# Linear attention and a snake MLP on one core: reading q of the first chunk in 2-KB rows

## The chip, the core and the metric

The kernel runs on one core of a Trainium2 chip. The core has a matrix engine (TensorE, "PE" in the profile; "PEld" is its loading of weights), a vector engine (VectorE, DVE), a scalar engine (ScalarE, ACT), GpSimd (POOL) and SyncE (SP). Each of them works through its own queue of instructions in order. Transfers between the chip's memory and the core's SBUF are issued by SP, ACT or POOL and carried out by 16 DMA engines that all of them share. TensorE writes its results to PSUM, eight banks of 512 fp32 columns in 128 partitions.

The metric is the device time of one execution in microseconds (us), the median of several runs.

## What is computed

Two stages follow one another. The first is a linear attention with decay, over 4 batches, 8 heads, 768 tokens and 64 features to a head, written for blocks of 64 tokens:

```python
for b in range(nb):
    intra = np.einsum('bhic,bhjc->bhij', qb, kb) * Dmask[None]
    intra = np.einsum('bhij,bhjd->bhid', intra, vb)
    inter = np.einsum('bhid,bhde->bhie', qb * lam_pow[None], kv_state)
    out[:, :, sl] = intra + inter
    kv_state = lam_block * kv_state + np.einsum('bhsd,bhse->bhde', kb * rev_pow, vb)
```

`Dmask`, `lam_pow` and `rev_pow` are powers of a decay `lam` that each head has for itself. The second is an MLP on the 3072 x 512 result (heads side by side), with 2048 hidden features:

```python
h = x @ w_in
s = np.sin(alpha * h)
g = h + s * s / (alpha + 1e-09)
return g @ w_out
```

All inputs and the output are fp32; the kernel works in bf16 with fp32 sums.

## The kernel before

The sequence is cut into six chunks of 128 tokens. For each chunk t the kernel makes `xt[t]`, the attention's output for the 4 x 128 tokens of all batches, with features in partitions; then the MLP's first half (`hidden`, 16 steps of four products of 512 columns, line 468), the snake (line 471 on ScalarE, line 485 on VectorE), and the second half (`project`, line 496), whose units are woven into the `hidden` steps of the next chunk. There is no scheduler: the order in the code is the order in each engine's queue.

Loads of q, k, v and the weights are issued by GpSimd, because they turn fp32 into bf16 on the way (`load`, lines 95 to 104; `load_w_in`, line 89; `load_w_out`, line 92). A load of one batch of q, k or v for one chunk puts tokens in partitions: partition p gets token p of eight heads, 64 features each, so it is 1024 pieces of 64 elements, 256 bytes read and 128 written. Batch 0's k and q come as fp32 through SP (line 81) and are cast on ScalarE and VectorE. Lines 112 to 120 issue, in this order: k and q of batches 1, 2 and 3, v of batches 0 to 3, `w_in` in two halves of its first quarter and then its three other quarters. `w_out`'s first quarter is issued in line 585, and the rest between the loads of the next chunk (lines 591, 629 and 630).

The first chunk has a code of its own (lines 544 to 582), with one mask over 128 tokens and no state yet. For each batch:

- `turn` (line 284) turns k and q with four transposes on TensorE (line 288) into one PSUM bank, of which they use half as bf16; ScalarE copies it to `QKT` (line 290). `turn_in_two` (line 277) does it for q of batch 0 with two copies. The layout wanted is features in partitions (two heads of 64 one above the other), four pairs of heads, 128 tokens in order.
- `scores1` (line 309) multiplies k and q of each head (line 313), and VectorE multiplies the sums with the decay mask `C0` into `STm` (line 317).
- `outs` multiplies with v (line 324), and ScalarE (batch 0, line 329) or VectorE (batches 1 to 3, with the decay `Etab`, line 331) writes `xt[0]`.

`spin` (line 127) issues products on a constant tile whose results nobody reads. Between these steps ScalarE works out small tables of powers of the decay: `decay_64` (`NE64` and `R64`, line 170), `decay_of_pair` (`L64`, line 195), `decay_128`, and `etab` (line 200). `mask_table` and `decay_k` on GpSimd, and the states of later chunks, use them.

At the end, `store` (line 500) copies a finished 128 x 512 tile out of PSUM and issues it on SP (`put_held`, line 514), in one transfer, or in two of 256 columns for the last chunk. The very last tile goes through `project_last` (line 516): 384 columns, a copy, two stores of 256 and 128 columns; then 128 columns, a copy, a store.

Of the kernel before, what the change touches and what calls it, by code (L numbers as in the profile page):

```python
# [15 lines left out]
def kernel(  # L16
# [11 lines left out]
    nc = tc.nc  # L28
    P = nc.NUM_PARTITIONS

    B, H, S, D = q.shape
    T = 128
    NT = S // T
    HP = H // 2
# [23 lines left out]
    def bank(nm, n, dtype=FP32):  # L58
        return psum.tile([P, 512 if dtype is FP32 else 1024], dtype, name=nm, tag=f"b{n}")
# [11 lines left out]
    qn, kn, vn = {}, {}, {}  # L71
    NAT = {"k": (kn, k), "q": (qn, q), "v": (vn, v)}

    def new_chunk(t):
        for d, nm, p in ((qn, "qn", qkp), (kn, "kn", qkp), (vn, "vn", vp)):
            d[t] = p.tile([P, B, H, D], BF16, name=nm)
# [18 lines left out]
    def load(t, nm, b0, b1):  # L95
        dst, src = NAT[nm]
        to = dst[t][:, b0:b1, :, :].rearrange("p b h e -> p (b h) e")
        by_head = src[b0:b1, :, t * T:(t + 1) * T, :].rearrange("b h p e -> p (b h) e")
        n = H * (b1 - b0)
        if t and nm != "v" and b0 == 2:  # L100
            nc.gpsimd.dma_start(out=to[:, 0:n - 1, :], in_=by_head[:, 1:n, :])  # L101
            nc.gpsimd.dma_start(out=to[:, n - 1:n, :], in_=by_head[:, 0:1, :])
        else:
            nc.gpsimd.dma_start(out=to, in_=by_head)  # L104

    new_chunk(0)
    new_chunk(1)

    dist = consts.tile([P, T], FP32, name="dist")
    nc.gpsimd.iota(out=dist[:], pattern=[[1, T]], base=0, channel_multiplier=-1,  # L110
                   allow_small_or_imprecise_dtypes=True)
    for nm, b0, b1 in (("k", 1, 2), ("q", 1, 2), ("k", 2, 3), ("q", 2, 3), ("k", 3, 4), ("q", 3, 4),
                       ("v", 0, 1), ("v", 1, 2), ("v", 2, 3)):
        load(0, nm, b0, b1)
    for hs in (slice(0, HP), slice(HP, H)):
        nc.gpsimd.dma_start(out=vn[0][:, 3, hs, :], in_=v[3, hs, 0:T, :].rearrange("h p e -> p h e"))  # L116
    load_w_in(0, 0, 2 * P)
# [9 lines left out]
    def spin(n, bk, cols=256):  # L127
        ps = bank("hps", bk)
        for _ in range(n):
            nc.tensor.matmul(out=ps[:, 0:cols], lhsT=fill[:, 0:P], rhs=fill[:, 0:cols], start=True, stop=True)  # L130

    iden = consts.tile([P, P], BF16, name="iden")
# [35 lines left out]
    def powers(nm, n, src, shape):  # L168
        t = consts.tile(shape, FP32, name=nm)
        nc.scalar.activation(out=t[:], in_=src, func=ACTF.Exp, scale=pcol[:, n:n + 1])  # L170
        return t
# [17 lines left out]
    def decay_64():  # L189
        later["NE64"] = powers("NE64", 3, lnlam[:].rearrange("p (hp hd) -> p hd hp", hd=2), [P, 2, HE])  # L190
        later["R64"] = powers("R64", 4, lnlam[:], [P, H + 2])

    def decay_of_pair(pr):
        for hd, half in enumerate(HALF):
            nc.scalar.activation(out=L64[half, pr, :], in_=lnlam[half, pr + hd:pr + hd + H - 1:2],
                                 func=ACTF.Exp, scale=float(D))
# [13 lines left out]
    V, G, A = nc.vector, nc.gpsimd, nc.scalar  # L210
    xt = {}
    kdec = {}
    KT, QT, both = {}, {}, {}
# [63 lines left out]
    def turn_in_two(t, b, n):  # L277
        ps = bank("T_ps", n, BF16)[:].rearrange("p (n c i) -> p n c i", n=2, c=HP)[:, 1]
        for hp in range(HP):
            nc.tensor.transpose(out=ps[:, hp, :], in_=qn[t][:, b, 2 * hp:2 * hp + 2, :], identity=iden[:])  # L280
        nc.scalar.copy(out=both[t][:, 1, b, 0:2, :], in_=ps[:, 0:2])
        nc.vector.tensor_copy(out=both[t][:, 1, b, 2:4, :], in_=ps[:, 2:4])

    def turn(t, nm, b, n, eng):
        src, u = (kn, 0) if nm == "k" else (qn, 1)
        ps = bank("T_ps", n, BF16)[:].rearrange("p (n c i) -> p n c i", n=2, c=HP)[:, u]
        for hp in range(HP):
            nc.tensor.transpose(out=ps[:, hp, :], in_=src[t][:, b, 2 * hp:2 * hp + 2, :], identity=iden[:])  # L288
        if eng is nc.scalar:
            eng.copy(out=both[t][:, u, b, :, :], in_=ps)  # L290
        else:
            eng.tensor_copy(out=both[t][:, u, b, :, :], in_=ps)
# [16 lines left out]
    def scores1(t, b, ns):  # L309
        Fb = [bank("F0_ps", n)[:].rearrange("p (c i) -> p c i", c=HP) for n in ns]  # L310
        for hp in range(HP):
            for hd in range(2):
                nc.tensor.matmul(out=Fb[hd][:, hp, :], lhsT=KT[t][halves(hd), b, hp, :],
                                 rhs=QT[t][halves(hd), b, hp, :], start=True, stop=True)
        st = work.tile([P, 2, HP, T], BF16, name="STm")
        for hd in range(2):
            nc.vector.tensor_tensor(out=st[:, hd], in0=Fb[hd], in1=C0[:, hd], op=ALU.mult)
        STm[t, b] = st
# [170 lines left out]
    held = []  # L489
# [10 lines left out]
    def store(g, m):  # L500
        o_sb = outp.tile([P, DM], FP32, name="o_sb")
        if g < NT - 2 and (g or m < 3):
            nc.vector.tensor_copy(out=o_sb[:], in_=ops_of.pop((g, m))[:])  # L503
        else:
            nc.scalar.copy(out=o_sb[:], in_=ops_of.pop((g, m))[:])  # L505
        held.append((m * S + g * T, o_sb, 2 if g == NT - 1 else 1))
        if g:
            put_held()

    def put_held():  # L510
        while held:
            row, o_sb, n = held.pop(0)
            for c in range(0, DM, DM // n):
                nc.sync.dma_start(out=out[row:row + T, c:c + DM // n], in_=o_sb[:, c:c + DM // n])

    def project_last(g, m):
        for n, (c, c1) in enumerate(((0, 3 * P), (3 * P, DM))):
            cols = slice(c, c1)
            ps = bank("hps", HB[n])
            for f in range(NFC):  # L520
                nc.tensor.matmul(out=ps[:, 0:c1 - c], lhsT=gall[g][:, f, m * P:(m + 1) * P],  # L521
                                 rhs=w_out_sb[f // 4][:, f % 4, cols],
                                 start=(f == 0), stop=(f == NFC - 1))
            o_sb = outp.tile([P, DM], FP32, name="o_sb")
            nc.scalar.copy(out=o_sb[:, 0:c1 - c], in_=ps[:, 0:c1 - c])
            row = m * S + g * T
            for c0 in range(c, c1, 2 * P):
                e = min(c0 + 2 * P, c1)
                nc.sync.dma_start(out=out[row:row + T, c0:e], in_=o_sb[:, c0 - c:e - c])

    new_xt(0)
    new_turned(0)
# [3 lines left out]
    def mask_128(hd):  # L536
        nc.vector.tensor_tensor(out=C0[:, hd], in0=tri[:].unsqueeze(1).broadcast_to([P, HP, T]),
                                in1=NE[:, hd].unsqueeze(2).broadcast_to([P, HP, T]), op=ALU.mult)
# [2 lines left out]
    nc.vector.tensor_tensor(out=qn[0][:, 0, :, :], in0=raw["q0"][:], op=ALU.mult,  # L541
                            in1=Rq[:].unsqueeze(2).broadcast_to([P, H, D]))
    mask_128(1)
    turn(0, "k", 0, 4, A)
    spin(2, 3)
    turn_in_two(0, 0, 5)
    spin(2, 3)
    turn(0, "k", 1, 1, A)
    scores1(0, 0, (6, 7))
    turn(0, "q", 1, 2, A)  # L550
    nc.sync.dma_start(out=alpha_fp[:], in_=moe_alpha.rearrange("(f p) -> f p", p=P))
    turn(0, "k", 2, 0, A)
    decay_64()
    spin(1, 3)
    scores1(0, 1, (4, 5))
    turn(0, "q", 2, 1, A)
    decay_of_pair(0)
    spin(1, 3)
    turn(0, "k", 3, 2, A)
    spin(1, 3)  # L560
    scores1(0, 2, (6, 7))
    turn(0, "q", 3, 0, A)
    a_ps = bank("a_ps", OB)
    nc.tensor.transpose(out=a_ps[:, 0:NFC], in_=alpha_fp[:], identity=idf[:])
    alpha_sb = consts.tile([P, NFC], FP32, name="alpha_sb")
# [40 lines left out]
    def queue_units(g, order):  # L606
        for m, part in order:
            def unit(g=g, m=m, part=part):
                project(g, m, part)
                if part == 3:  # L610
                    store(g, m)
            behind.append(unit)
# [69 lines left out]
    def slots(g):  # L682
        t = g + 1
        d = {i: [] for i in range(NFC)}
        if g == 1:
            at = dict(KV=5, F=9, O=12)
        else:
            at = dict(KV=4, F=8, O=12)
        d[at["KV"]] += [(states, t)]
        for n in range(4):  # L690
            d[at["KV"] + ((0, 0, 1, 2)[n] if g == 1 else n)] += [(update, t, n // 2, n % 2)]
        if g == 1:
            d[8] += [(run, 1), (scores, 2), (masks, 2, 0)]
        else:
            d[at["F"]] += [(scores, t), (masks, t, 0)]
        d[at["F"] + (g > 1)] += [(masks, t, 1)]
        d[at["O"]] += [(outputs, t), (leave, t, 0)]
        d[at["O"] + (g > 1)] += [(leave, t, 1)]
        return d
# [21 lines left out]
    for g in range(1, NT + 1):  # L721
        if g < NT:
            gall[g] = gbp.tile([P, NFC, GRP], BF16, name="gall")
        at = slots(g) if g + 1 < NT else {}
# [21 lines left out]
        if g < NT:  # L746
            queue_units(g, [(m, part) for m in range(B - 1 if g == NT - 1 else B) for part in range(4)][len(own):])
    project_last(NT - 1, B - 1)


# [28 lines left out]
```

## Time and profile before

| | us |
|---|---|
| three runs: median (lowest, highest) | 208.51 (208.45, 209.97) |
| the profiled execution's own time | 209.9 |
| its span in the trace | 208.1 |
| TensorE busy in the span | 200.0 (96%) |
| ScalarE, VectorE, GpSimd busy | 143.2, 131.3, 108.8 |

Times of rows are counted from the span's start. The span is shorter than the execution's own time by what lies before and after it. A row of the timeline gives start and length in us, the engine, the line, what is written and read, how many instructions were merged, and in brackets the idle time before them with what ended it. A busy TensorE is not TensorE at its peak, since products overlap in its pipeline: the end of the last of a group lies some 0.2 us behind the start of the next.

### The profile page before, as it was taken

What the parts mean: (1) busy time and instruction counts of PE and PEld (TensorE: products, weight loads), DVE (VectorE), ACT (ScalarE), POOL (GpSimd) and SP (SyncE); (2) the same over time, 40 slices, a digit from 0 to 9 for tenths busy, and PEclk for the clock granted to TensorE, in tenths of its full rate; (3) what the DMA queues carried; (4) which work ended last, traced back from release to release, by engine and by line L of the source; (5) the groups of instructions that cost most, each with busy time, mean ns of one, the idle gap of its engine ahead of it and who ended that gap; (6) DMA issues with size and microseconds to landing.
All of it is one profiled execution on the core that took longest, in us unless ns stands there. A gap on an engine that the chain in (4) does not pass through costs nothing.

```text
span 208.1 us, 5352 instructions
## 1 busy us (share of the span) xinstructions
PE 200.0 (96%) x2232; PEld 98.0 (47%) x2232; DVE 131.3 (63%) x218; ACT 143.2 (69%) x241; POOL 108.8 (52%) x114
## 2 busy tenths in 40 slices
PE   7997999979999999999999999999999999999993
PEld 2653445544454544445444444445444444444442
DVE  7792898563698969968557967556867544444000
ACT  7695998222989799775776675776675787887121
POOL 8999949998979992999976840002000000000000
PEclk9999999999999999999999999999999999999999
DMA  8999999999999999599999949701101101110213
GB/s 129 152 154 187 202 165 182 175 187 157 141 208 168 145 128 162 85 176 162 117 153 164 200 77 136 170 0 54 50 3 54 50 0 50 52 54 0 101 53 100
DMA packets 99402, 24.47 MB, mean 118 GB/s; under 512 B 91042, under 2 KB 96818, under 8 KB 99378
## 3 DMA queue, kind: packets, MB, share of 16 engines
q0 software_dynamic: 77248, 13.37, 85.3%
q1 hardware_dynamic: 22128, 10.76, 26.2%
q8 instruction: 17, 0.28, 0.5%
q14 instruction: 7, 0.06, 0.1%
q10 hardware_dynamic: 2, 0.00, 0.0%
HBM read 27.27 MB, written 6.29 MB: 161 GB/s over the span
## 4 chain that ended last, share of the span: by engine, by line
PE 77%; POOL 12%; DMA 9%; issue 0%; ACT 0%; POOLq 0%; ACTq 0%
PE ops L496 36%; PE hps L468 34%; DMA kn<-in_k_dram 5%; DMA w_out<-in_moe_w_out_dram 4%; POOL kdec L242 3%; PE O_ps L418 2%; POOL w_in L89 2%; PE hps L521 2%; PE F_ps L404 1%; POOL kn L104 1%; POOL qn L104 1%; POOL vn L104 1%; PE KV_ps L384 1%; PE O_ps L443 1%; POOL vn L116 1%; POOL qn L101 1%
## 5 line engine op out<-in xcount | busy, mean ns | idle before, releaser
L485 DVE SCALAR_TENSOR_TENSOR gall<-s,r_sb,hps 128x512 bf16<-128x512 bf16 x96 | 71.0, 744 | 45.7 <-ACT s L476 45.5
L468 PE MATMUL hps<-xt,w_in 128*128 128x512 bf16 x384 | 95.8, 379 | 1.6 <-DMA w_in<-in_moe_w_in_dram 1.6
L496 PE MATMUL ops<-w_out,gall 128*128 128x512 bf16 x368 | 92.1, 379 | 1.3 <-DMA w_out<-in_moe_w_out_dram 1.3
L471 ACT ACTIVATE s_sb<-hps,alpha_sb 128x512 bf16<-128x512 f32 x96 | 65.3, 684 | 33.0 <-PE hps L468 32.8
L476 ACT ACTIVATE s<-s_sb 128x512 bf16<-128x512 bf16 x91 | 57.3, 629 | 2.9
L468 PEld LDWEIGHTS <-w_in 128*128 128x128 bf16 x384 | 36.5, 98 | 44.5 <-DMA w_in<-in_moe_w_in_dram 2.3
L496 PEld LDWEIGHTS <-gall 128*128 128x128 bf16 x368 | 34.7, 98 | 42.2 <-issue 2.0
L242 POOL TENSOR_TENSOR kdec<-kn,R 128x1024 bf16<-128x1024 bf16 x12 | 22.9, 1941 | 4.5 <-DMA kn<-in_k_dram 4.5
L353 POOL CAST sb<-S 128x512 bf16<-128x512 f32 x20 | 12.3, 621 | 20.6 <-DVE S L360 20.6
L349 POOL TENSOR_TENSOR SD<-S,L 128x512 f32<-128x512 f32 x16 | 16.7, 1049 | 9.1 <-DVE S L360 8.9
L450 DVE TENSOR_TENSOR xt<-O_ps,Etab 128x512 bf16<-128x512 f32 x20 | 12.8, 683 | 6.2 <-PE O_ps L443 6.2
L104 POOL DMA_DIRECT2D vn<-in_v_dram x13 | 14.7, 1139 | 0.0
L411 DVE TENSOR_TENSOR STm<-F_ps,C 128x512 bf16<-128x512 f32 x20 | 12.8, 681 | 1.3 <-PE F_ps L404 1.3
L503 DVE COPY o_sb<-ops 128x512 f32<-128x512 f32 x15 | 10.3, 689 | 4.2 <-PE ops L496 4.1
L505 ACT COPY o_sb<-ops 128x512 f32<-128x512 f32 x8 | 4.6, 577 | 12.0 <-PE ops L496 12.0
L360 DVE TENSOR_TENSOR S<-SD,KV_ps 128x512 f32<-128x512 f32 x16 | 10.8, 682 | 0.1
L130 PE MATMUL hps<-fill 128*128 128x256 bf16 (+1 forms) x29 | 7.9, 380 | 1.5 <-DVE fill L123 1.5
L104 POOL DMA_DIRECT2D kn<-in_k_dram x8 | 8.8, 1098 | 0.3 <-issue 0.3
L104 POOL DMA_DIRECT2D qn<-in_q_dram x8 | 8.6, 1081 | 0.0
L290 ACT COPY QKT<-T_ps 128x512 bf16<-128x512 bf16 x9 | 5.0, 588 | 4.1 <-PE T_ps L288 4.1
L418 PEld LDWEIGHTS <-sb 64*64 64x64 bf16 x320 | 4.3, 108 | 4.8 <-issue 4.7
L101 POOL DMA_DIRECT2D kn<-in_k_dram x5 | 6.2, 1247 | 0.0
(79 smaller groups left out, 114.5 us busy)
## 6 DMA issues: line engine op xcount, KB each, us to landing
out_dram<-o_sb SPq DMA_DIRECT2D x20, 256.0 KB, 2.4
vn<-in_v_dram POOLq DMA_DIRECT2D x10, 256.0 KB, 7.7
w_out<-in_moe_w_out_dram POOLq DMA_DIRECT2D x4, 512.0 KB, 11.6
w_in<-in_moe_w_in_dram POOLq DMA_DIRECT2D x3, 512.0 KB, 10.4
kn<-in_k_dram POOLq DMA_DIRECT2D x5, 256.0 KB, 7.6
qn<-in_q_dram POOLq DMA_DIRECT2D x5, 256.0 KB, 9.6
kn<-in_k_dram POOLq DMA_DIRECT2D x5, 240.0 KB, 7.6
qn<-in_q_dram POOLq DMA_DIRECT2D x5, 240.0 KB, 8.7
```

Source lines behind the costliest of these rows:

```text
L104: nc.gpsimd.dma_start(out=to, in_=by_head)
L242: nc.gpsimd.tensor_tensor(out=kdec[t][:, b0:b1, :, :], in0=kn[t][:, b0:b1, :, :], in1=R[:, o:o + H].unsqueeze(1).unsqueeze(3).broadcast_to ...
L349: nc.gpsimd.tensor_tensor(out=pair(SD, pr), in0=pair(S_of[n], pr), op=ALU.mult, in1=L64[:, pr].unsqueeze(1).unsqueeze(3).broadcast_to([P, ...
L353: nc.gpsimd.tensor_copy(out=pair(dst, pr), in_=pair(S_of[n], pr))
L360: nc.vector.tensor_tensor(out=S, in0=pair(SD, pr), in1=ps, op=ALU.add)
L411: nc.vector.tensor_tensor(out=st[:, hd], in0=att["F", t, pr, hd], op=ALU.mult, in1=of_mask(C64, t, pr, hd).unsqueeze(1).broadcast_to([P, 2 ...
L450: nc.vector.tensor_tensor(out=xview(t)[:, 2 * pr:2 * pr + 2, blk, :, :], in0=att["O", t, pr, blk], in1=Eb, op=ALU.mult)
L468: nc.tensor.matmul(out=hps[:], lhsT=w[:, c, (f % 4) * P:(f % 4 + 1) * P], rhs=xt[g][:, c, :], start=(c == 0), stop=(c == NDC - 1))
L471: nc.scalar.activation(out=s_sb[:], in_=hps[:], func=ACTF.Sin, scale=alpha_sb[:, f:f + 1])
L476: nc.scalar.activation(out=s2[:], in_=s_sb[:], func=ACTF.Square)
L485: nc.vector.scalar_tensor_tensor(out=gall[g][:, f, :], in0=s2[:], scalar=r_sb[:, f:f + 1], in1=hps[:], op0=ALU.mult, op1=ALU.add)
L496: nc.tensor.matmul(out=ops[:], lhsT=gall[g][:, f, m * P:(m + 1) * P], rhs=w_out_sb[part][:, f % 4, :], start=(f == 0), stop=(f == NFC - 1))
```

## The change

Loads: q of batches 1 to 3 of the first chunk is read by `load_q_rows`. With `E8` = 8, the 128 tokens of a head are 16 groups of eight; partition n * 8 + h gets group n of head h, which is eight rows of 64 elements in one piece of 2 KB of fp32, 1 KB as bf16. That is 128 pieces in place of 1024. The order of the loads is the same.

Turning: `turn_rows` brings this layout into the same `QKT` as before. For each of the eight tokens of a group and each half of the head pairs it issues a product with a 128 x 64 slice of the loaded tile as the weights and 64 columns of the identity as the moving operand; the columns are picked in steps of eight elements (16 bytes), and the 64 sums are written in steps of eight fp32 columns (32 bytes), so the tokens come out in order. Sixteen products replace four transposes, the bank holds fp32 and is used whole, and one copy on ScalarE takes it out.

Order: in the first chunk's code `decay_64` and `decay_of_pair(0)` go ahead, to before the copy of the first turned k and to behind those of batch 0's q; two `spin` calls of one product go; the turn of batch 3's q stands before the scores of batch 2 instead of behind them.

Stores: `project_last` stores its 384 columns at once; the tile of the last batch of the last chunk but one is stored in two halves.

```diff
+    E8 = T * H // P
+    def q_rows(b):
+        return qn[0][:, b].rearrange("p h d -> p (h d)")
+    def load_q_rows(b):
+        nc.gpsimd.dma_start(out=q_rows(b), in_=q[b, :, 0:T, :].rearrange("h (n e) d -> n h (e d)", e=E8))
...
-    for nm, b0, b1 in (("k", 1, 2), ("q", 1, 2), ("k", 2, 3), ("q", 2, 3), ("k", 3, 4), ("q", 3, 4),
-                       ("v", 0, 1), ("v", 1, 2), ("v", 2, 3)):
-        load(0, nm, b0, b1)
+    for b in range(1, B):
+        load(0, "k", b, b + 1)
+        load_q_rows(b)
+    for b in range(3):
+        load(0, "v", b, b + 1)
...
+    iden_of = iden[:].rearrange("p (n c k) -> p k c n", c=HP, k=2)
+    def turn_rows(b, n):
+        ps = bank("T_ps", n)[:]
+        at = ps.rearrange("p (c n e) -> p e c n", c=HP, e=E8)
+        for e in range(E8):
+            for hd in range(2):
+                nc.tensor.matmul(out=at[hd * D:(hd + 1) * D, e], lhsT=q_rows(b)[:, e * D:(e + 1) * D],
+                                 rhs=iden_of[:, hd], start=True, stop=True)
+        nc.scalar.copy(out=both[0][:, 1, b, :, :], in_=ps.rearrange("p (c i) -> p c i", c=HP))
...
-        held.append((m * S + g * T, o_sb, 2 if g == NT - 1 else 1))
+        held.append((m * S + g * T, o_sb, 2 if g * B + m >= (NT - 1) * B - 1 else 1))
...
-            for c0 in range(c, c1, 2 * P):
-                e = min(c0 + 2 * P, c1)
-                nc.sync.dma_start(out=out[row:row + T, c0:e], in_=o_sb[:, c0 - c:e - c])
+            nc.sync.dma_start(out=out[row:row + T, cols], in_=o_sb[:, 0:c1 - c])
...
+    decay_64()
     turn(0, "k", 0, 4, A)
     spin(2, 3)
     turn_in_two(0, 0, 5)
     spin(2, 3)
+    decay_of_pair(0)
     turn(0, "k", 1, 1, A)
     scores1(0, 0, (6, 7))
-    turn(0, "q", 1, 2, A)
+    turn_rows(1, 2)
...
     turn(0, "k", 2, 0, A)
-    decay_64()
     spin(1, 3)
     scores1(0, 1, (4, 5))
-    turn(0, "q", 2, 1, A)
-    decay_of_pair(0)
-    spin(1, 3)
+    turn_rows(2, 1)
     turn(0, "k", 3, 2, A)
-    spin(1, 3)
+    turn_rows(3, 0)
     scores1(0, 2, (6, 7))
-    turn(0, "q", 3, 0, A)
```

## The prediction

> **What bounds the kernel now.** I read the page first, for the span and the load on the DMA engines.
>
> ```profile
> span 208.1 us, 5352 instructions
> DMA  8999999999999999599999949701101101110213
> ```
>
> The 16 DMA engines are almost always busy in the first 40% of the span. Next comes the chain of waits (start, length, what), followed back from the end; of its rows these matter:
>
> ```profile
> 20.17 10.27 DMA kn<-in_k_dram
> 35.73 9.11 DMA w_out<-in_moe_w_out_dram
> 44.88 1.02 PE ops L496 x4
> ...
> 205.00 0.27 ACT o_sb L525
> ```
>
> Up to 44.88 us the end hangs on the transfers that GpSimd issues, and from there on TensorE runs without a gap that the chain shows until the last copy at 205.00. TensorE's own waits between 16 and 46 us agree. Only two are listed:
>
> ```profile
> PE hps L468 <- DMA w_in<-in_moe_w_in_dram: 1.6, 1, 1.6
> PE ops L496 <- DMA w_out<-in_moe_w_out_dram: 1.3, 1, 1.3
> ```
>
> So the question is when w_out's third quarter lands, the wait that ends at 44.88. The windows view (last columns: DMA share, which counts overlapping packets and so passes 1, and GB/s written) says whether the queue ever empties before that:
>
> ```profile
> 5.00:13.00 8.00, 7.49 (x91) 5.21 (x92) 6.35 (x12) 6.22 (x18) 8.00 (x11) 1.00 2.58 150
> 14.00:17.00 3.00, 1.40 (x19) 0.76 (x16) 1.73 (x5) 1.83 (x4) 3.00 (x3) 1.00 1.22 153
> 18.00:25.00 7.00, 7.00 (x47) 3.10 (x46) 5.03 (x9) 6.79 (x12) 7.00 (x7) 1.00 1.24 205
> 28.00:31.00 3.00, 2.92 (x15) 1.14 (x13) 2.96 (x6) 2.81 (x5) 0.49 (x1) 1.00 2.44 156
> 35.00:39.00 4.00, 4.00 (x55) 2.09 (x54) 4.00 (x10) 1.66 (x3) 4.00 (x7) 1.00 2.40 159
> ```
>
> It doesn't. From 28 to 31 us a backlog is certain (GpSimd issues nothing, and k of the next chunk lands 10.27 us after its issue); there the engines write 156 GB/s in q, k and v's 128-byte pieces mixed with weights. From 5 to 13 us, where only such pieces move, it is 150: the engines are full there already. From 18 to 25 us, with w_in's and w_out's 1024-byte pieces, it is 205. One queue, never empty, and TensorE waiting for a transfer at its end: time taken out of the front of the queue comes off the end of the kernel, as long as TensorE arrives in time.
>
> **The change, part by part.**
>
> *q in 2-KB rows.* Each of the three loads writes 128 KB, before in 1024 pieces of 128 bytes, after in 128 pieces of 1024. At 150 GB/s that is 0.87 us of the engines, at 205 it is 0.64: 0.235 saved, three times 0.70 us. GpSimd has to keep up for this to show. Its rows:
>
> ```profile
> L104 POOL DMA_DIRECT2D qn<-in_q_dram x3 | 2.7, 903 | 0.0
> L102 POOL DMA_DIRECT2D kn<-in_k_dram x2: 572/632/693, 25.6 to 47.5; - x2
> L102 POOL DMA_DIRECT2D qn<-in_q_dram x2: 580/588/597, 35.2 to 50.4; - x2
> ```
>
> An issue of 1024 pieces takes 0.90 us; one with a single piece in each of 128 partitions (L102) 0.59 to 0.63. The new loads have one piece in each partition, so GpSimd is 3 x 0.27 to 0.31 = 0.8 to 0.95 us earlier at v and the weights behind them. The smaller of the two, 0.70, is what I take. From below it is 0.07 if the new pieces go at the 153 GB/s of w_in's first half (512-byte pieces, 14 to 17 us); from above 3 x 0.87 = 2.6 if they cost nothing. The 205 is nearest: same piece size, same cast from fp32 to bf16. In a sentence beside it: "DMA: Bandwidth & Descriptors" of the Trainium skill, section Specifications, puts the least size for line rate at 512 B; it would give the whole gain to 512-byte pieces already, while this trace has 153 GB/s there and 205 only at 1024.
>
> *Does TensorE arrive in time?* The rows of TensorE and VectorE around its start:
>
> ```profile
> 8.15 5.48 DVE L317 TENSOR_TENSOR STm<-F_ps,C 128x512 bf16<-128x512 f32 x8 [0.68 <-PE F_ps L313]
> 13.55 2.02 DVE L331 TENSOR_TENSOR xt<-O_ps,Etab 128x512 bf16<-128x512 f32 x4
> 16.91 1.90 PE L468 MATMUL hps<-xt,w_in 128*128 128x512 bf16 x8 [1.60 <-DMA w_in<-in_moe_w_in_dram]
> ```
>
> VectorE has no gap from 8.15 to 15.57, where xt is ready; TensorE starts at 16.91, when w_in lands. With w_in 0.70 earlier it starts at 16.2, still behind xt by 0.6. Everything up to w_out's third quarter moves by 0.70, and the wait of 1.26 before 44.88 stays. If TensorE started no earlier at all it would still reach that wait at 43.6, before 44.88 - 0.70 = 44.18. So xt may come 1.34 + 0.56 = 1.9 us late before any of the 0.70 is lost: that is the cover for all that follows.
>
> *The new turning.* Sixteen products of 64 columns in alternating halves of the array replace four of 128 columns, and two of the three spins between go. Nearest rows:
>
> ```profile
> 18.75 0.44 PE L341 MATMUL KV_ps<-vn,kdec 128*64 128x64 bf16 x16
> 19.12 0.39 PE L468 MATMUL hps<-xt,w_in 128*128 128x512 bf16 x1
> 8.04 0.40 PE L288 MATMUL T_ps<-iden,qn 128*128 128x128 bf16 x4
> 8.28 0.39 PE L288 MATMUL T_ps<-iden,kn 128*128 128x128 bf16 x4
> L288 PE MATMUL T_ps<-iden,qn x12: 219/219/230, 8.0 to 11.0; 128*128 128x128 bf16 x12
> ```
>
> Sixteen such products hold the queue 0.37 us (18.75 to 19.12), 23 ns each, and end after 0.44; four transposes hold it 0.24 and end after 0.40. So each turn is ready 0.04 later and blocks 0.13 longer. The third now stands ahead of batch 2's scores, which wait in TensorE's queue behind it:
>
> ```profile
> 9.93 0.40 PE L288 MATMUL T_ps<-iden,kn 128*128 128x128 bf16 x4
> 10.17 0.27 PE L130 MATMUL hps<-fill 128*128 128x256 bf16 x1
> 10.52 0.40 PE L313 MATMUL F_ps<-QKT 64*128 64x128 bf16 x8
> 5.88 0.92 POOL L104 DMA_DIRECT2D qn<-in_q_dram  x1
> qn<-in_q_dram POOLq DMA_DIRECT2D x1, 128.0 KB, 4.9
> ```
>
> Before, q of batch 3 lands at 5.88 + 4.9 = 10.8; after, 0.7 earlier, at 10.1. The spin ahead of k's turn (0.25) is gone, so that turn ends its hold near 10.1, the rows' turn runs 10.1 to 10.5, and the scores start near 10.55 instead of 10.52. VectorE then stalls by under 0.1 us; if q came no earlier at all it would be 0.65. Either is inside the 1.9. What no row shows is a product that reads its moving operand in steps of 16 bytes and writes its sums in steps of 32, as these do. From below it is the 23 ns of contiguous operands (sixteen can hardly go faster); from above the 219 ns that one transpose takes from end to end (the fifth row above), if nothing overlaps: 48 x 0.196 = 9.4 us. I take a value near the row, which has the same 64 columns and the same alternation.
>
> *Copies and small tables on ScalarE.* The copy out of fp32 sums takes 0.57 by a cast of the same shape (the first row below) where the copies below it take 0.59: no change. The tables follow:
>
> ```profile
> L329 ACT CAST xt<-O_ps 128x512 bf16<-128x512 f32 x1 | 0.6, 570 | 0.0
> 5.92 0.59 ACT L290 COPY QKT<-T_ps 128x512 bf16<-128x512 bf16 x1 [0.70 <-PE T_ps L288]
> 7.62 0.59 ACT L290 COPY QKT<-T_ps 128x512 bf16<-128x512 bf16 x1 [0.48 <-PE T_ps L288]
> 9.44 0.32 ACT L170 ACTIVATE NE<-lnlam,pcol 128x10 f32<-128x10 f32 x1
> 9.64 0.30 ACT L170 ACTIVATE R<-lnlam,pcol 128x10 f32<-128x10 f32 x1
> 10.36 0.42 ACT L195 ACTIVATE L<-lnlam 64x4 f32<-64x4 f32 x2
> ```
>
> NE and R (9.44 to 9.88 with the overlap, 0.44) go into the idle 0.70 before 5.92, L (0.42) into the 0.48 before 7.62. Both fit, the second with 0.06 to spare; without that cover the scores of batch 1 start that much later, again inside the 1.9. In their old place they stood between copies that batch 2's scores wait for, so ScalarE gains 0.86 us of room, and what is late next there is the DMA and TensorE's turn, as above.
>
> *The stores.*
>
> ```profile
> L529 SPq DMA_DIRECT2D out_dram<-o_sb x3: 332/409/433, 204.6 to 205.5; - x3
> DMA to landing us min/median/max: 1.7/1.7/1.7
> out_dram<-o_sb SPq DMA_DIRECT2D x20, 256.0 KB, 2.4
> ```
>
> The last of three issues starts at 205.5, though its data is there at 205.27. With two, SP is free at 205.0 and the last starts at about 205.3: 0.2 us off the end, as the landing takes the same 1.7. The first store grows to 192 KB; even at the 2.4 us of a 256-KB store it lands no later than the last. The store that is split in two 10 us earlier adds one issue of 0.4 us to a queue that mostly waits for copies: nothing.
>
> **Sum:** 0.70 + 0.20 = 0.90 us. The profiled execution took 209.9 us around its span of 208.1; it would become 209.0 around 207.2. The three runs before have the median 208.51, 1.4 below the profiled one; the same 0.9 gives 207.6.
>
> **Rivals.**
>
> *Dear strided products (slower).* "SBUF — State Buffer" of the Trainium skill, section "Door 1: The DMA port swizzle", says that accesses which step to a new 16-byte line each time pay a penalty and that any non-contiguous access in PSUM slows matmuls significantly. No run so far has such a product, so it speaks against this change. Worked out from the rows: each ns above 23 costs 48 ns ahead of xt, since VectorE has no gap. The 1.9 us of cover, less 0.1 for the stall, are used up at 23 + 1800/48 = 60 ns a product. The whole 0.9 is lost at 79 ns, and 1% (2.1 us) is lost at 123. At 110 ns the kernel takes 210.0 us. For it: the pattern is as bad as can be. Against: four times the price is needed before anything is lost. 0.11.
>
> *The change doesn't shorten the queue.* The engines may pay for reading 256 KB of fp32, not for pieces, as the 153 GB/s of w_in's first half hints, or w_out's issue is held by GpSimd's other work. Then only the stores count: 208.3. Against: 205 against 150 in saturated stretches. 0.17.
>
> *More than the queue's 0.70.* If q's loads cost nothing, w_in lands before xt, TensorE starts at 15.7 and reaches w_out 1.2 us earlier, at 42.4, when it has just landed: at most 1.2 + 1.26 + 0.2 = 2.7, 205.8. Over 1% (2.1) would need 1.9 from the queue, 0.24 us for a load, which is 546 GB/s; the best stretch has 205. Between, say 1.4 in all, 207.1: GpSimd's 0.95 and a lower latency at the front. 0.14.
>
> **Numbers.** The forecast (206.9 to 208.1, about half of the 0.70 either way) has 0.58. I call 1% (2.1 us) what a measurement here can tell from no change, as the three runs before spread over 1.5 us. Over 1% faster: a third of the last rival, 0.05, and 0.02 for what I have overlooked. Over 1% slower: half of the strided rival, 0.06, and 0.02 beside it. Within: 0.85. The range 206.6 to 209.0 takes in the forecast, the unshortened queue, most of the third rival and the mild half of the strided one.
>
> **What would show it.** In the profile after: q's issues at 0.6 us; w_in's wait ending near 16.2 and w_out's near 44.2; each turn's sixteen products holding TensorE's queue about 0.4 us; VectorE without a gap over 0.1 us from 8.15 to 15.6; two last stores. The prediction is wrong if xt is ready later than 17.5, if w_out's wait doesn't move with w_in's, or if the dense part after it is no longer as long.

## The result, and the profile after

| | before | after |
|---|---|---|
| median of 14 runs each, us | 208.82 | 207.97 |
| lowest to highest | 208.45 to 210.27 | 207.61 to 208.26 |
| ratio after / before, 95% interval | | 0.995 (0.9934 to 0.9965) |
| profiled execution: its time, its span | 209.9, 208.1 | 208.26, 206.3 |

The change makes the kernel 0.85 us faster, 0.5%. The two profiles differ by more, 1.8 us of span, because the profiled execution of before was a long one, 1.1 us over the median of its runs. A second profile of before, below, helps to see which of its waits are typical.

The chain of waits of the changed kernel (start, length, what):

```profile
7.98 1.05 PE T_ps L300 x16
10.09 1.03 PE T_ps L300 x16
11.45 1.03 PE T_ps L300 x16
12.86 1.95 DVE STm L337 x4
15.25 1.62 DVE xt L351 x3
17.43 1.46 PE hps L488 x6
43.47 1.13 DVE S L384 x4
```

Before, up to 44.88 us, the chain ran over GpSimd's issues and the transfers. Now no transfer is on it: TensorE's new products, VectorE's masks and xt carry the front, and near 43 us VectorE's update of the state. TensorE's waits between 0 and 60 us say the same. No row names a DMA:

```profile
PE ops L516 <- issue: 0.3, 2, 0.2
PE hps L488 <- DVE xt L351: 0.3, 1, 0.3
PE F_ps L333 <- ACT QKT L302: 0.2, 1, 0.2
```

And TensorE and VectorE around the MLP's start, from the timeline:

```profile
7.91 1.10 PE L300 MATMUL T_ps<-iden,qn 128*64 128x64 bf16 x16
8.94 0.40 PE L308 MATMUL T_ps<-iden,kn 128*128 128x128 bf16 x4
10.11 1.29 DVE L337 TENSOR_TENSOR STm<-F_ps,C 128x512 bf16<-128x512 f32 x2 [0.80 <-PE F_ps L333]
12.85 2.48 DVE L337 TENSOR_TENSOR STm<-F_ps,C 128x512 bf16<-128x512 f32 x4 [1.45 <-PE F_ps L333]
15.25 1.94 DVE L351 TENSOR_TENSOR xt<-O_ps,Etab 128x512 bf16<-128x512 f32 x4
17.00 1.89 PE L488 MATMUL hps<-xt,w_in 128*128 128x512 bf16 x7 [0.28 <-DVE xt L351]
```

Sixteen products hold TensorE from 7.91 to 8.94, 1.03 us or 64 ns each, where the forecast had 23. VectorE, which had no gap in the profile of before, waits 0.80 us for the scores of batch 1 and 1.45 us for those behind the third turn. So xt is ready at 17.19 in place of 15.57, and TensorE's MLP starts at 17.00, before the last piece of xt is written, no earlier than before (16.91), although w_in's first half now lands at 15.4.

The queue did get shorter. In the windows view of the changed kernel (DMA share and GB/s in the last columns) the engines write 168 GB/s in the front stretch and 202 from 14 to 17 us, against 150 and 153 before:

```profile
5.00:13.00 8.00, 7.76 (x100) 5.80 (x100) 4.55 (x9) 5.08 (x13) 8.00 (x12) 1.00 2.02 168
14.00:17.00 3.00, 2.73 (x43) 1.64 (x42) 3.00 (x7) 2.89 (x7) 1.51 (x2) 1.00 1.32 202
```

So two readings were open. In the first, the queue theory, the forecast holds: the landing of w_out sets the end, and the dear products are covered. In the second, the turning theory, the products now set the front, and making them cheap would bring more.

### The profile page after: what moved, and what is told of

It is laid out like the page before. It is cut to its first block, busy times and chain, and to the rows that moved or that the text cites. A ratio compares the mean times of both kernels' runs of the same rounds, so it can differ in the third digit from the quotient of the medians.

```text
span 206.3 us, 5390 instructions
## 1 busy us (share of the span) xinstructions
PE 199.3 (97%) x2236; PEld 99.6 (48%) x2266; DVE 131.0 (63%) x218; ACT 143.1 (69%) x241; POOL 107.8 (52%) x114
## 4 chain that ended last, share of the span: by engine, by line
PE 93%; DVE 3%; issue 2%; ACT 0%; DVEq 0%; ACTq 0%
PE hps L488 40%; PE ops L516 38%; PE O_ps L438 2%; PE hps L139 2%; PE hps L541 2%; PE T_ps L300 2%; PE F_ps L424 1%; PE KV_ps L404 1%; PE O_ps L463 1%; DVE STm L337 1%; PE T_ps L308 1%; DVE xt L351 1%; PE T_ps L322 1%; PE F_ps L333 1%; DVE S L384 1%
## 5 line engine op out<-in xcount | busy, mean ns | idle before, releaser
L488 PE MATMUL hps<-xt,w_in 128*128 128x512 bf16 x369 | 94.2, 379 | 1.3 <-issue 0.3
L516 PE MATMUL ops<-w_out,gall 128*128 128x512 bf16 x353 | 90.3, 379 | 0.9 <-issue 0.3
L369 POOL TENSOR_TENSOR SD<-S,L 128x512 f32<-128x512 f32 x16 | 16.7, 1050 | 9.8 <-DVE S L380 9.7
L431 DVE TENSOR_TENSOR STm<-F_ps,C 128x512 bf16<-128x512 f32 x20 | 12.8, 683 | 0.0
L139 PE MATMUL hps<-fill 128*128 128x256 bf16 (+1 forms) x27 | 7.4, 388 | 1.5 <-DVE fill L132 1.5
L337 DVE TENSOR_TENSOR STm<-F_ps,C 128x512 bf16<-128x512 f32 x8 | 5.1, 685 | 2.8 <-PE F_ps L333 2.8
L101 POOL DMA_DIRECT2D qn<-in_q_dram x5 | 6.2, 1233 | 0.0
```

Source lines behind the costliest of these rows:

```text
L369: nc.gpsimd.tensor_tensor(out=pair(SD, pr), in0=pair(S_of[n], pr), op=ALU.mult, in1=L64[:, pr].unsqueeze(1).unsqueeze(3).broadcast_to([P, ...
L431: nc.vector.tensor_tensor(out=st[:, hd], in0=att["F", t, pr, hd], op=ALU.mult, in1=of_mask(C64, t, pr, hd).unsqueeze(1).broadcast_to([P, 2 ...
L488: nc.tensor.matmul(out=hps[:], lhsT=w[:, c, (f % 4) * P:(f % 4 + 1) * P], rhs=xt[g][:, c, :], start=(c == 0), stop=(c == NDC - 1))
L516: nc.tensor.matmul(out=ops[:], lhsT=gall[g][:, f, m * P:(m + 1) * P], rhs=w_out_sb[part][:, f % 4, :], start=(f == 0), stop=(f == NFC - 1))
```

## The experiments

**A second profile of before.**

> The kernel before once more, for a second profile: the one shown took 209.9 us, 1.1 over the median of its runs since. If the 1.26-us wait for w_out's third quarter belongs to slow executions, it is 0.0 to 0.5 us here and the span near 207.0; if it is always there, 1.0 to 1.5 us.

Measured: 209.27 us, span 207.5, which is still 0.4 us over the median of before on that chip (208.84). Its waits of TensorE, and the rows around the MLP's start:

```profile
PE ops L496 <- DMA w_out<-in_moe_w_out_dram: 1.6, 2, 1.4
PE hps L468 <- DVE xt L331: 0.3, 1, 0.3
13.82 2.02 DVE L331 TENSOR_TENSOR xt<-O_ps,Etab 128x512 bf16<-128x512 f32 x4
15.87 1.90 PE L468 MATMUL hps<-xt,w_in 128*128 128x512 bf16 x8 [0.28 <-DVE xt L331]
```

The wait for w_out's third quarter is there again (1.38 us). But w_in isn't what TensorE starts on: it lands 5.0 us after its issue at 10.80, at 15.8, and TensorE starts at 15.87, with xt. The 1.34 us of slack between xt and w_in, which the forecast read from one execution, are not there in every execution.

**The price of a product: which step?** Three versions of the changed kernel, run on one chip.

The moving operand flat:

```diff
+    idp = consts.tile([P, P], BF16, name="idp")
+    iden_by = idp[:].rearrange("p (k c n) -> p k c n", k=2, c=HP)
...
-                                 rhs=iden_of[:, hd], start=True, stop=True)
+                                 rhs=iden_by[:, hd], start=True, stop=True)
...
+    nc.vector.tensor_copy(out=iden_by, in_=iden_of)
     mask_128(0)
```

> The changed kernel, with the identity's columns copied once into a table in the order in which they are read (one 128x128 copy on VectorE in its idle time before the masks), so the moving operand is contiguous; the sums are still written in steps of 32 bytes. In the changed kernel a product holds TensorE 64 ns and xt is ready at 17.2 us, after w_in (15.4). If the step of the moving operand is the price: 23 to 30 ns a product, 48 x 35 = 1.7 us off the front, xt near 15.6. Queue theory (the forecast): the time stays at the changed kernel's, 0.85 us under before, since w_out's third quarter sets the pace. Turning theory: the front now sets the end, 1.0 to 2.2 us under before. If the step of the sums is the price: 64 ns and no change under both.

The sums flat:

```diff
-        at = ps.rearrange("p (c n e) -> p e c n", c=HP, e=E8)
+        at = ps.rearrange("p (e c n) -> p e c n", c=HP, e=E8)
...
-        nc.scalar.copy(out=both[0][:, 1, b, :, :], in_=ps.rearrange("p (c i) -> p c i", c=HP))
+        nc.scalar.copy(out=both[0][:, 1, b, :, :].rearrange("p c (n e) -> p c n e", e=E8),
+                       in_=ps.rearrange("p (e c n) -> p c n e", c=HP, e=E8))
```

> The changed kernel, with each product writing 64 contiguous fp32 columns; ScalarE's copy out of the bank puts the tokens in order, so it reads PSUM in steps of 256 bytes. The moving operand is still read in steps of 16 bytes. If the step of the sums is the price: 23 to 30 ns a product, and 1.0 to 2.2 us under before by the turning theory, 0.85 by the queue theory; the copy may take longer than its 0.58 us (up to 1.2), which would give three times the difference back. If the moving operand is the price: 64 ns, 0.85 us under before or less.

Both edits together:

> Both together: contiguous moving operand, contiguous sums, the order made by the copy. 23 to 27 ns a product if no other cause is left. Queue theory: 0.85 us under before, as the changed kernel. Turning theory: 1.0 to 2.2 us under before, with TensorE's first step of the MLP at 15.7 to 16.0 in place of 17.0, and a wait for w_out's third quarter coming back in part.

The timeline of TensorE has the first turn of each, a row with the sixteen products and the row of the transposes that follow. First the moving operand flat:

```profile
7.80 0.64 PE L303 MATMUL T_ps<-idp,qn 128*64 128x64 bf16 x16
8.37 0.40 PE L311 MATMUL T_ps<-iden,kn 128*128 128x128 bf16 x4
```

The sums flat:

```profile
7.74 1.10 PE L300 MATMUL T_ps<-iden,qn 128*64 128x64 bf16 x16
8.77 0.40 PE L309 MATMUL T_ps<-iden,kn 128*128 128x128 bf16 x4
```

Both flat, with TensorE's first step of the MLP:

```profile
7.73 0.44 PE L303 MATMUL T_ps<-idp,qn 128*64 128x64 bf16 x16
8.11 0.40 PE L312 MATMUL T_ps<-iden,kn 128*128 128x128 bf16 x4
15.36 1.90 PE L492 MATMUL hps<-xt,w_in 128*128 128x512 bf16 x7
```

The distance of the two starts, divided by sixteen, is the price of a product:

| version | ns a product | time, us | ratio to before (95%) |
|---|---|---|---|
| as changed | 64 | 207.97 | 0.995 (0.9934 to 0.9965) |
| sums flat | 64 | 207.84 | 0.9946 (0.9923 to 0.997) |
| moving operand flat | 36 | 207.53 | 0.9929 (0.9903 to 0.9956) |
| both flat | 24 | 207.37 | 0.9917 (0.9887 to 0.9947) |
| both flat, second time | | 207.46 | 0.9931 (0.9913 to 0.9949) |

The moving operand's step is the larger price, though taking it away alone leaves 36 ns and not the 23 to 30 expected; the sums' step shows only once that one is gone. In these four versions the slower of the two rates holds, they don't add. ScalarE's copy takes 0.58 to 0.60 us in all of them, so the reading in steps costs nothing there. Both flat takes 1.4 and 1.6 us less than before in two runs on one chip, where the queue theory had 0.85: as far as the changed kernel goes, the turning theory holds. On another chip the changed kernel took 207.77 to 208.35 us and both flat with the tables at their old places (below) 207.09 to 207.65. The expectation for the second run of both flat was:

> Both flat once more, as the measure for the next two on the same chip: 207.2 to 207.6 us, 1.4 to 1.8 under before.

The front moved by 1.64 us (17.00 to 15.36), the span of these two profiles by 0.8 and the medians by 0.5 to 0.6. What took up the rest shows in both flat's waits for weights to be loaded (an answer over 14 to 60 us): the transfers are back.

```profile
PEld L492 <- DMA w_in<-in_moe_w_in_dram: 0.6, 2, 0.4
PEld L312 <- DMA qn<-in_q_dram: 0.5, 1, 0.5
PEld L520 <- DMA w_out<-in_moe_w_out_dram: 0.5, 1, 0.5
```

The same can be read from ScalarE's operations in line 471 of before, one to each step of `hidden`. From the first of them to the first of the second chunk the two profiles of before take 33.7 and 34.1 us, the changed kernel's 32.1, and both flat's 32.9 and 32.5; from there to the end of the last copy each of these takes 153.5 to 153.7. So the whole difference lies in when the MLP starts and in the waits of its first chunk, and the changed kernel, which starts late, has none left.

**The loads alone, and the turning alone.** First the changed kernel with `turn(0, "q", b, n, A)` in place of `turn_rows(b, n)`:

> The changed kernel with the four plain transposes in place of the sixteen products: the loads in 2-KB rows, the moved tables and the stores are kept, and the step that puts the tokens of batches 1 to 3 of q back in order is left out. Queue theory: as the changed kernel, 0.85 us under before. Turning theory: as both flat, 1.0 to 2.2 us under before, xt near 15.6. If the loads had no part in the gain: 0.2 us under before, by the stores alone.

Measured: 207.43 us, ratio 0.9919 (0.9891 to 0.9947), as both flat. Its profile gets there in another way than expected: TensorE starts at 16.46 and not near 15.6, since in that execution VectorE waited 0.76 us for q of batch 0 (until 6.09 us), and no wait of TensorE for a transfer follows. Then the changed kernel with `load(0, "q", b, b + 1)` in place of `load_q_rows(b)`, beside the changed kernel on the same chip:

> The changed kernel once more, as the measure for the other three on the same chip: 0.7 to 1.1 us under before, products of 64 ns, xt at 17.2 us in the profile, no wait for w_out of over 0.3 us.

> The changed kernel with q of batches 1 to 3 loaded as before, in 256-byte pieces, and turned by the sixteen products all the same; the output's order of tokens for these batches of the first chunk is then not made. It has the dear products, the moved tables and the stores without the shorter queue. Queue theory (the gain is the queue's): the gain is gone, 0.0 to 0.3 us under before, w_in landing near 16.8 and w_out's wait back. Turning theory for the front: xt at 17.5 to 18.0, so TensorE starts 0.6 to 1.1 us later than before and the wait for w_out shrinks by as much; the end is then at before's, or up to 0.5 later where before hardly waits for w_out. If the loads had no part in the gain: as the changed kernel.

Measured: the changed kernel 208.01 us, ratio 0.993 (0.9905 to 0.9956); without the row loads 208.77, ratio 0.9981 (0.9959 to 1.0003). So the loads bring 0.76 us with the dear products, and the rest of the change 0.3, about what the stores bring (below). That 0.3 isn't clear of noise, as the interval shows. The dear products cost nothing that these runs can tell while the queue is long: in that run's profile w_in lands at 16.5, TensorE starts at 16.52 with xt not yet complete (16.68, where 17.5 to 18.0 was expected), and it sits idle for w_out only 0.2 us, with 0.6 us each in the loading of weights for w_out and for q. So the queue theory's cover is real with the old loads. With the shorter queue there is less of it.

**What shortens the queue: the engines' time or GpSimd's?** The rows of GpSimd and of the landings (KB, us from issue) for w_in's first issues and w_out's first quarter. In the second profile of before:

```profile
10.80 3.82 POOL L89 DMA_DIRECT2D w_in<-in_moe_w_in_dram  x5
w_in<-in_moe_w_in_dram POOLq DMA_DIRECT2D x1, 256.0 KB, 5.0
14.46 0.90 POOL L92 DMA_DIRECT2D w_out<-in_moe_w_out_dram  x1
w_out<-in_moe_w_out_dram POOLq DMA_DIRECT2D x1, 512.0 KB, 13.3
```

And in the second profile of the changed kernel, with the length of the new issues first:

```profile
L114 POOL DMA_DIRECT2D qn<-in_q_dram x3: 537/545/546, 2.4 to 5.2; - x3
9.84 3.77 POOL L89 DMA_DIRECT2D w_in<-in_moe_w_in_dram  x5
w_in<-in_moe_w_in_dram POOLq DMA_DIRECT2D x1, 256.0 KB, 5.0
13.49 0.85 POOL L92 DMA_DIRECT2D w_out<-in_moe_w_out_dram  x1
w_out<-in_moe_w_out_dram POOLq DMA_DIRECT2D x1, 512.0 KB, 13.6
```

Each issue is 0.36 us shorter, and w_in is issued 0.96 us earlier and lands 0.96 us earlier (15.80 to 14.84). Over the three profiles with the old loads w_in's first half lands at 15.8 to 16.9 and w_out's first quarter at 27.7 to 28.5; in ten with the new ones (all but the next test) it is 14.9 to 15.8 and 26.6 to 27.6. The means differ by 1.1 at both places. With scatter of that size the landings alone don't tell 0.96 from 0.70. The test was to give GpSimd its time back and leave the engines the cheap pieces:

```diff
+    pad = consts.tile([P, 192], FP32, name="pad")
     for b in range(1, B):
         load(0, "k", b, b + 1)
         load_q_rows(b)
+        nc.gpsimd.tensor_tensor(out=pad[:, 0:P], in0=dist[:], in1=dist[:], op=ALU.add)
```

> Both flat (1.4 to 1.6 us under before), with a GpSimd operation of about 0.3 us that nobody reads (a 128x128 fp32 sum) behind each of the three row loads, so that GpSimd reaches v and w_in about as late as before (w_in's first issue near 10.8 in place of 9.84) while the DMA engines keep the cheaper pieces. If the queue's shift is GpSimd's earlier issue: w_in's first half lands near 16.3 in place of 15.3 and w_out's first quarter near 28 in place of 27.1, the time 0.3 to 0.8 us over both flat. If it is the engines' saved time (the forecast's 0.70): they land less than 0.4 us later, the time 0.0 to 0.2 over both flat.

The delay came out larger than meant: the operations took 0.41, 0.81 and 0.41 us.

```profile
11.52 3.75 POOL L89 DMA_DIRECT2D w_in<-in_moe_w_in_dram  x5
w_in<-in_moe_w_in_dram POOLq DMA_DIRECT2D x1, 256.0 KB, 5.1
15.19 0.82 POOL L92 DMA_DIRECT2D w_out<-in_moe_w_out_dram  x1
w_out<-in_moe_w_out_dram POOLq DMA_DIRECT2D x1, 512.0 KB, 14.3
```

With w_in issued 1.68 us later it lands 1.4 us later (16.7 against 15.3 in both flat), w_out's first quarter 2.7 later (29.5 against 26.8), and the kernel takes 209.56 us, ratio 1.0028 (1.0005 to 1.0051). All of both flat's gain is gone, and more: 2.0 to 2.3 us by the ratios, where 0.3 to 0.8 was expected. The issue is now 0.72 us later than in before, k's turns wait as well in that run (0.8 us), and one quarter of w_in lands 3.6 us behind the transfer ahead of it where both flat has 2.5; what each of these is worth was not taken apart. What the run does show is that with a late issue the engines' saved time does not keep the gain.

The landings at the front fit this. In the first profile of before the nine loads of k, q and v from 1.33 to 8.48 us each land 4.7 to 5.0 us after their issue (4.7 to 5.4 in the second), so hardly any backlog builds up: 131 KB every 0.87 us, or 151 GB/s, is what GpSimd issues there. The engines are not far from their own limit, since in the changed kernel's profile the same pieces go at 152 to 159 GB/s from 27 to 29 us, behind a certain backlog. The opposite test, an early issue with dear pieces, was not made, and a version with q in 512-byte pieces gave no result. So how much of the gain would be left without the engines' saved time is open.

**The stores.** The changed kernel with the old stores:

> The changed kernel with the old stores: three in the last tile, one for the tile that is split now. The forecast's term: 0.2 us slower than the changed kernel. If the last landing hides it: the same.

Measured: 208.32 us, ratio 0.9964 (0.9938 to 0.9989), 0.31 over the changed kernel of the same chip; the intervals overlap. The rows of the last store's issues, with the old stores and in the changed kernel:

```profile
L549 SPq DMA_DIRECT2D out_dram<-o_sb x3: 332/401/424, 202.8 to 203.7; - x3
```

```profile
L547 SPq DMA_DIRECT2D out_dram<-o_sb x2: 332/332/332, 202.9 to 203.6; - x2
203.31 0.27 ACT L545 COPY o_sb<-hps 128x128 f32<-128x128 f32 x1 [0.42 <-PE hps L541]
```

With two stores the last is issued as its data is there (203.58); with three it waits 0.2 us behind the second (in that run the data is there at 203.48, and the issue starts at 203.7).

**The tables.** Both flat, with `decay_64` and `decay_of_pair(0)` at their old places:

> The version with both operands flat (1.6 us under before), with the small tables at their old places between the copies. ScalarE then stands in front of batch 2's and 3's scores by up to 0.86 us. If the moved tables matter once the products are cheap: xt 0.3 to 0.8 us later than 15.27, 0.1 to 0.6 us slower than both flat. If VectorE's chain covers them: the same, 1.6 us under before.

Measured: 207.33 us, ratio 0.9906 (0.9873 to 0.994). Once the products are cheap, moving the tables has no effect that these runs show: xt comes at 15.45 in place of 15.27, and w_in lands then anyway (15.4). Both flat itself was not run on that chip, so the comparison goes by the ratios (0.9917 and 0.9931).

**The same for the next chunk.** Both flat, with q of batches 0 and 1 of the second chunk loaded and turned in the same way, and the copies on VectorE:

> Both flat, and q of batches 0 and 1 of the second chunk read and turned in the same way (two loads in 2-KB rows, sixteen flat products each, fp32 copies that order the tokens, on VectorE). In both flat TensorE waits for that q, 0.5 us up to 30.9, behind a full queue. If the queue is still the bound there: 0.2 to 0.6 us faster than both flat. If TensorE and VectorE are now the bound: two turns of 0.38 in place of 0.24 and two copies of 0.6 to 0.7 in place of 0.4 stand on the chain, 0.1 to 0.8 us slower.

Measured: 207.85 us, ratio 0.9952 (0.9935 to 0.9968), 0.39 slower than both flat on that chip, though the intervals overlap. The wait for that q, 0.5 and 0.2 us in the two profiles of both flat, is gone from its trace. But 32 products hold TensorE for 0.63 us (31.21 to 31.84) where eight transposes held it 0.44 to 0.46, and VectorE's two copies, now from fp32, take 1.29 us in place of 0.76. How the 0.39 divides between them was not tested. Here the turn pays at the front, where TensorE waits for transfers anyway, and not in the dense part.

## Why the prediction was right, and where it wasn't

The forecast was 207.6 us, 0.90 faster than its median of before; measured were 207.97 us and 0.85. That the two are so near is partly luck: two of its terms were mis-sized in opposite directions, and one reading was taken from a single execution. Of the signs that it named, q's short issues (0.55 to 0.57 us) and the two last stores came, and the dense part is as long as before (154.1 us from the first copy of a finished tile to the last, in both profiles). The waits for w_in and w_out at their new times, the turns of 0.4 us and a VectorE without gaps did not come.

- *The queue.* That time taken out of the front of the queue comes off the end was right. With cheap products the kernel gains 1.4 to 1.6 us, 1.1 to 1.3 without the stores, and the queue moves by some 1.1: about one for one, as forecast. The size was wrong, and most likely the choice of what sets it. The forecast took "the smaller of the two", the engines' 0.70; w_in's landing followed GpSimd's 0.8 to 0.95 (measured 0.96). The 150 GB/s from 5 to 13 us looked like full engines, but k, q and v were also issued at just that rate. The lower bound misread a row, too: the 153 GB/s from 14 to 17 us was not the price of 512-byte pieces. In the changed kernel's profile w_in's same pieces go at 193 to 206 GB/s there, as fast as 1024-byte ones; what held them back before is open. (The bound itself comes to 0.05 us, not 0.07.)
- *The products.* This step failed: 64 ns in place of 23. The forecast had the pattern as a rival and priced it: cover used up at 60 ns, so 0.2 us lost at 64. The runs show 0.5 to 0.7 lost (207.97 or 208.01 against 207.33 to 207.46 for both flat, with and without the moved tables). The likely reason is that the cover was smaller than 1.9: its 1.34 us between xt and w_in belonged to one execution, the second profile of before has none of it, and a queue that is 1.1 shorter leaves less than one that is 0.70 shorter. The sentence of "SBUF — State Buffer" in the Trainium skill, section "Door 1: The DMA port swizzle", that a step to a new 16-byte line each time has a price agrees with these runs, 64 against 36 ns with the sums still in steps. Its other half, on PSUM, agrees with the moving operand flat, 36 against 24; with the moving operand in steps the sums' step costs nothing more (64 and 64).
- *w_out's wait.* It was to stay at 1.26 and move by 0.70. It went away: TensorE came later than forecast and w_out's third quarter earlier (42.1 us in the second profile of the changed kernel, 34.14 + 8.0, against 44.15 in that of before, 34.95 + 9.2). What was late next is xt at the front and VectorE's state near 43 us. The third quarter moved by more than the queue's front did; with the old loads and the new turning it was early, too (35.76 + 7.7 = 43.5). Part of this is how it shares the engines with the fourth quarter behind it. In both profiles of before the third lands 3.2 to 3.3 us behind q and the fourth 2.0 to 2.1 later; with the old loads and the new turning it is 2.6 and 2.5, nearly the same together. Why it falls out one way or the other is left open.
- *Copies, tables, stores.* As forecast: 0.58 us for the copy, no effect of the tables, 0.2 us for the stores in the trace (0.31 in the medians).

The products' price was that of the strided rival, which had a chance of 0.11, at its mild end. The time still came out near the forecast because the rest of the change was worth 0.5 to 0.7 us more than forecast.

## What to carry to other kernels

When a queue of transfers looks full, compare its rate with the rate at which it is issued, and see whether the time from issue to landing grows. Where the rates are equal and it hardly grows, as here, no backlog builds up, and a later or earlier issue moves the landing. Give the moving operand of a small product a contiguous table of its own: one copy of 0.3 us here took 28 ns off each of 48 products, and writing the sums in one piece another 12. And read slack that is to hide a new cost from two executions: waits for transfers near the start moved by 1 us from one to the next here.

## What the runs showed of the hardware beside that

The prices of two stepped operands of one product don't add: 64 ns with both or with the moving one, 36 with the sums alone, 24 with neither. A GpSimd issue of 128 pieces takes 0.54 to 0.57 us where a piece writes 1024 bytes and 0.57 to 0.71 where it writes 128, and one of 1024 pieces of 128 bytes about 0.90: the count of pieces matters more than their bytes. And with the same issue times w_in's first half landed at 15.3 us in one profile of both flat and at 15.8 in another, and at 15.8 and 16.9 in the two of before: 0.5 to 1 us of this landing is chance.
